# One set of PSUM banks, one order, one late pass for the low rows, and Strassen's products for batch 1 and the low rows

## The chip, the cores and the metric

The kernel runs on one core of a Trainium2 chip. The engines of that core are TensorE (PE in the profile, with its weight loads as PEld), VectorE (DVE), ScalarE (ACT), GpSimd (POOL) and SyncE (SP, which issues most DMAs). They run side by side and wait for each other by semaphores. The metric is the time of one execution on the device, in microseconds (us); lower is better.

## The reference

Two stages, for 8 batches. First an attention between 512 rows `x` and 32 rows `state` in 8 heads of width 64, in both directions; the results of both directions stand below each other, 544 rows of 512 values (the heads side by side) for each batch. Then a block of Fourier mixing with a two-layer network:

```python
scores  = scale * x @ state.T;  a  = softmax(scores);   xread = a @ state
scores2 = scale * state @ x.T;  a2 = softmax(scores2);  sread = a2 @ x
x = concat([xread, sread])                 # 544 rows of 512, per batch
u  = x + real(fft(fft(x, axis=rows), axis=columns))
un = (u - mean(u)) / sqrt(var(u) + 1e-6)   # per row
out = u + relu(un @ w_ch1) @ w_ch2         # 512 -> 2048 -> 512
```

All inputs and the output are float32.

## The kernel before

**Tiles and stages.** For each batch the 544 rows are 4 tiles of 128 rows and 32 rows more, the low rows (each batch has 32; the low rows of four batches make a tile of 128). A batch goes through: scores, transposed scores, reads of the state (`attend`, or `open_batch` for batch 0); the Fourier transform over the rows, made of products with cosine and sine tables (`over_s`, result tiles gp and G); the transform over the columns (`over_d`, `second_axis`, result yp); the sum U with the input; centring (ub) and transposing (unT); layer 1 (`layer1`: ph, then relu into hT); layer 2; and U plus the scaled result (ot), which is stored. Rows that have to be mirrored go by a buffer in DRAM (r_dram); low rows by l_dram.

**Layer 2** exists in two forms. `layer2` multiplies each 128-row tile of hT with w2: 16 matmuls of 512 columns into one bank po, then one step of VectorE. `layer2_fast` takes a pair of row tiles and treats hT (256 x 2048) and w2 (2048 x 512) as 2 x 2 blocks with Strassen's scheme in Winograd's form: seven products of 8 matmuls with 256 columns each instead of eight. For this it needs sums on both sides. The weight sums T1 to T4 are made once (`weight_sum`, VectorE). The sums of hT are made for each pair: S1 (tile SA), S2 (SB), and two that replace blocks of hT in place. The products gather in the banks poA and poB, and seven steps of VectorE (`put`) add them into ot. Before the change, batches 0 and 1 and the low rows use `layer2`, and batches 2 to 7 use `layer2_fast`.

**The low rows** are worked on twice: those of batches 0 to 3 in the step b = 3 of the main loop, those of batches 4 to 7 in b = 7 (`low_rows(g4)`), each with a pass of layer 1 (matmuls of 128 columns, tile unTL, result hTL) and of layer 2 of its own.

**Banks.** [...] The opening (batch 0's attention and its first transform) takes them from a pool ps0. After it the pool is closed, and psX (2 banks), psQ (3) and psF (3) are opened. At b = 3 these are closed again, and psX (2), psq (2) and psf (4) follow. BANKS says which bank each tile takes.

**Order.** The code doesn't issue instructions directly: a `Recorder` gathers them in groups, and `play` issues the groups in an order written out by hand or by a planner (ORDERS). `play` is called three times, so that there are three stretches: 0 (the opening, in the order of the code), 1 (up to b = 3) and 2 (the rest). No instruction moves across these borders. Groups of one key follow one another: the key of a TensorE instruction is the name of the tile that it writes.

**The opening**, ahead of which nothing runs: GpSimd makes index tables and clears buffers; VectorE and ScalarE turn them into the cosine and sine tables; SyncE and ScalarE load x of batch 0; TensorE fills its waits with small products that nobody reads (`warm`). Then come scores, exponentials (EE), reads, the fold of rows and columns (Sm, SS, XO0), the products gp, yp, U and ub. The first half of ub goes to ScalarE, the second to VectorE.

Every operation is issued by one helper, so the profile shows all at one line (L63); the tiles' names tell them apart.

Of the kernel before, what the change touches and what calls it, by code (L numbers as in the profile page):

```python
# [12 lines left out]
F32 = mybir.dt.float32  # L13
BF16 = mybir.dt.bfloat16
# [6 lines left out]
class Recorder:  # L21
# [4 lines left out]
    def __init__(self, nc):  # L26
        self.nc, self.groups, self.stretch = nc, [], 0
        for name in self.ENGINES:
            setattr(self, name, _Engine(self, name, getattr(nc, name)))
# [10 lines left out]
    def play(self):  # L40
        order = ORDERS.get(self.stretch) or range(len(self.groups))
        assert sorted(order) == list(range(len(self.groups)))
        for n in order:
            for call in self.groups[n][1]:
                made = call()
                if HOOK:
                    HOOK(self.stretch, n, made)
        self.groups, self.stretch = [], self.stretch + 1


class _Engine:
# [3 lines left out]
    def __getattr__(self, what):  # L55
        f = getattr(self._engine, what)
        if not callable(f):
            return f

        def call(*args, **kw):  # L60
            out = kw.get("out", args[0] if args else None)
            key = out.tensor.name if self._name == "tensor" else None
            self._rec.add(self._name, lambda: f(*args, **kw), key)  # L63

        return call


ORDERS = {n: [i for p in t.split() for i in range(int(p.split("-")[0]), int(p.split("-")[-1]) + 1)] for n, t in {
    1: """
        1-2 35 4 0 3 5-6 42 33 7 20 10 84 9 12-13 28 22 25 24 27 23 143 26 29 32 40 39 51 34 36 41 147 227 37 52-54 93 38 45 49  # L70
        57 50 58 43 61 87 63 55 46 62 64-65 47 70 105 48 71-72 88-89 148 18 73 123 76 80 21 82 11 15 209 74-75 19 78 16 210 77
        79 17 124-126 132 83 59 90 103 68 94 98 91-92 99 229 100 96 66 107 56 60 44 69 95 106 97 104 67 108-112 119-120 113 121
        118 114-116 152 117 145 157 165 159 161 101 85 175 182 167 173 169 158 146 166 160 162 102 176 168 174 170 86 171 180
        186 179 189 163 181 188 183-184 193 197 202 198 201 187 190 153 228 211 206 151 156 150 207 154 191 149 212 230 172 185
        164 199 195 200 224 222 235 194 203 215 218 223 295 196 208 192 81 283 14 122 281 130 279 128 231 213 232 129 233 214
        220 155 216 135 134 31 133 30 136 139-141 138 142 137 204 236 225 205 226 237 285 234 282 177 127 249 242 238 256 239
        245 296 243 287 240 246 244 251 250 221 144 262 252 261 260 253 259 265 450 255 254 263 451 266 302 270 288 267-269 286
        273 272 275 274 276 280 277-278 290 293 332 304 247 307 310 257 291-292 305-306 297 301 298 300 299 311-315 318-319 321
        320 323 327-328 324 330 309 374 326 334 339 337 316 335 322 329 341 343 346 241 303 271 178 333 294 248 308 325 375 331
        338 340 317 336 342 344 354 363 348 378 370 351 350 365 349 379 366 356-357 372-373 390-391 371 385 355 347 364 383 352  # L80
        361 381 384 353 386 369 382 360 394 389 397 362 217 258 264 455 377 376 396 395 449 454 431 402-403 411 404-405 419 430
        420 407 437 443 423 399 406 401 8 400 367 414 413 387 398 284 392 412 417-418 131 416 415 427 425 429 426 219 428 424
        289 446 478 456 421-422 409 444 432 436 445 435 439 457-458 434 433 459-461 472 474 469 464 468 465-466 473 467 537 481
        448 475 462 441 480 470 490 476 495 499 486 497 507 493 483 488 447 479 482 463 442 471 477 500 496 487 494 502 552 515
        550 510 527 549 511 557 542 485 509 491 503 518 504-506 517 519 516 558 556 498 484 508 489 553 524 532 551 539 531 523
        512-514 543 545 501 525 358-359 388 533 540 546-547 368 345 526 393 534 541 554 520 528 560 535 492 380 453 452 544 410
        522 530 538 559 438 440 408 529 521 561 536 555 548
    """,
    2: """
        38 2 13 0 12 4 1 36 8 97 22 32 5 61 9-10 37 39 14 23-24 98 62 46 11 15 17 16 19 18 21 20 44 63 131 65 56 53 33-34 42 7 6  # L90
        25 64 111 79 67 26 29 54-55 57 43 78 68 80 69 41 40 59 70 72 71 73-75 92 76 93 60 94 52 84 89 50 85 88 35 58 241 240 49
        47 82 48 83 51 86-87 30 104 113 99 175 95 90 123 106 115 102 119 117 125 45 183 132 112 31 77 96 103 120 110 108 121 188
        141 105 66 114 176 91 124 116 107 118 126 100 122 189 142 148 163 133 185 190 128 151 149-150 134 152 135-136 109 101
        225 177 138 145 143 161 200 144 129 137 164 154 191 186 140 178 139 146 155 147 201-202 158 208 162 166-167 221 217 174
        184 187 236 192 239 242 273 170 277 243 165 153 179 130 271 274-275 244-245 276 414 301 303 250 350 269 256 283 246 285
        223 203 159 204-205 212 210 27-28 211 213 168 215 214 156 216 226 218-219 209 222 230 206 227 237-238 194 229 263 228
        251 220 207 252-253 255 254 258-259 278 260 280 233 248 235 267-268 279 261-262 234 305 231 291 297 309 299 281 295 298
        249 282 304 171 351 270 257 284 361 286 224 180 247 306 232 292 300 302 296 264 311 287 320 342 265 313-314 366 362 330
        325 373 316 344 293 328 310 327 288 312 321-322 308 323-324 345 326 343 318 367 334 363 374 331 317 294 338 329 160 266
        272 332 195 356 399 364 358 368 169 413 157 379 315 380 394 359 357 319 369 333 197 416 290 352 337 360 346 193 415 417  # L100
        419 418 422 395 375 381 423 365 409 376-377 441 383 378 385 384 127 386 389 388 390 387 172 181 173 307 182 438 391 370
        407 392 371 393 396 408 439 443 410 397 509 448 468 424 450 470 528 444 398 510 339 347 451 469 471 411 400-401 412 403
        402 425-426 449 437 404 427-429 432 436 433 442 434 445 447 446 460 497 454 430 405 464 420 455 465 435 458 476 466 472
        492 462 461 431 406 498 459 353 467 473 421 463 523 452 487 540 478 529 535 533 511 477 475 489 488 490 480 479 491
        493-494 512 481-482 524 453 541 536 505 500 534 486 485 440 457 519 513 504 499 372 542 566 531 525 483 495 558 517 530
        484 496 518 501 543-544 532 526 567 348 354 335 545 551 336 502 474 340 553 355 557 552 554 349 556 341 503 555 537 577
        548 590 584 603 580 628 562 641 665 568 571 570 559 569 560 578 546 579 506 591 604 581 550 538 585-587 597 547 589 588
        593 605 574 610 572 564 582 592 561 563 607 575-576 594 596 583 595 606 618 673 624 622 598 630 626 608 625 601-602 599
        609 629 682 642 514 666 520 611 565 573 619 623 631 627 645 650 614 636 692 634 620 653 667 646-649 633 615 638 651 637
        635 639 652 640 668 656 674 661 693 643 621 644 654 657 662 515 521 632 516 699 685 679 683 686 701 700 689 612 687 456  # L110
        539 549 527 669 675 289 660 196 655 670 684 676 688 613 780 720 703 737 696 705 786 707 680 690 694-695 702 708 698 704
        711 507 677 671 658 678 663-664 659 522 508 709 672 710 718 712 748 713 719 725 714-715 729 722 730 723 81 681 617 691
        697 382 199 717 198 3 721 738 781 787 706 749 733 772 743 770 759 766 755 761 746 777 741 783 745 726 734 754 742 773
        744 716 771 767 762 756 760 778 784 739 731 750 727 752 757 747 753 758 768-769 732 740 751 728 801 774 779 782 798 785
        788 796 800 775 797 805 799 802 790 724 736 600 735 776 616 789 791 806 763 803 807 811 764 816 804 808 813 817 809 815
        812 821 810 814 822 819 823 818 820 824-826 833 827 831 834 828 836-837 765 794 793 792 835 795 829 839 830 840 838 832
        841
    """,
}.items()}
BANKS = {  # L120
    "psQ":
        "210002012201120210210201120120221012000022121021",
    "psF":
        "1220102100210012220120212011120210020012002110100101102212",
# [8 lines left out]
HOOK = None  # L133
# [1419 lines left out]
```

## Time and profile before

| | us |
|---|---|
| median of three runs | 294.81 |
| lowest and highest | 293.24, 295.10 |
| the profiled execution | 294.75 |
| its span, from the first to the last instruction | 293.0 |

| engine | busy us | share of the span | instructions |
|---|---|---|---|
| TensorE | 280.3 | 96% | 2599 |
| TensorE weight loads | 193.1 | 66% | 2599 |
| VectorE | 207.0 | 71% | 530 |
| ScalarE | 164.7 | 56% | 323 |
| GpSimd | 98.1 | 33% | 227 |

The span is the part of the time that the trace covers; 1.75 us lie around it. A share of busy time is a mean over stages, so it is read together with the row that cuts the span into 40 slices and with the chain of waits, which follows the work that ended last back to the start. A row of a group of instructions gives its busy time, the mean duration of one in ns, and the idle time of the engine ahead of them with what ended it. Matmuls overlap, so their mean duration is longer than their spacing; the spacing is read from the chain.

### The profile page before, as it was taken

What the parts mean: (1) busy time and instruction counts of PE and PEld (TensorE: products, weight loads), DVE (VectorE), ACT (ScalarE), POOL (GpSimd) and SP (SyncE); (2) the same over time, 40 slices, a digit from 0 to 9 for tenths busy, and PEclk for the clock granted to TensorE, in tenths of its full rate; (3) what the DMA queues carried; (4) which work ended last, traced back from release to release, by engine and by line L of the source; (5) the groups of instructions that cost most, each with busy time, mean ns of one, the idle gap of its engine ahead of it and who ended that gap; (6) DMA issues with size and microseconds to landing.
All of it is one profiled execution on the core that took longest, in us unless ns stands there. A gap on an engine that the chain in (4) does not pass through costs nothing.

```text
span 293.0 us, 6742 instructions
## 1 busy us (share of the span) xinstructions
PE 280.3 (96%) x2599; PEld 193.1 (66%) x2599; DVE 207.0 (71%) x530; ACT 164.7 (56%) x323; POOL 98.1 (33%) x227
## 2 busy tenths in 40 slices
PE   5997999999999999999999999999999999999993
PEld 4677987554654546677764867767666866768682
DVE  8878696449579955895569795986787964613772
ACT  6984755764763696346845647276766584253000
POOL 6762683628057127600243011611273106000000
PEclk9997999999999999999999999999999999999998
DMA  9999499599934547855356034721352058640655
GB/s 159 190 203 212 77 154 110 115 172 163 196 80 103 101 121 140 180 121 140 66 118 127 25 94 123 120 72 39 70 122 61 22 107 187 136 110 0 130 160 143
DMA packets 110972, 34.91 MB, mean 119 GB/s; under 512 B 101996, under 2 KB 106476, under 8 KB 110940
## 3 DMA queue, kind: packets, MB, share of 16 engines
q1 hardware_dynamic: 100220, 28.72, 47.0%
q0 software_dynamic: 4224, 4.19, 9.2%
q10 hardware_dynamic: 6496, 1.57, 2.6%
q8 instruction: 20, 0.33, 0.5%
q14 instruction: 12, 0.10, 0.1%
HBM read 22.41 MB, written 14.02 MB: 124 GB/s over the span
## 4 chain that ended last, share of the span: by engine, by line
PE 72%; DVE 10%; SPq 6%; DMA 4%; POOL 3%; ACT 1%; issue 1%; DVEq 0%; POOLq 0%
PE ph L63 31%; PE poA L63 14%; PE poB L63 10%; PE po L63 7%; SPq L63 6%; PE gp L63 3%; PE yp L63 2%; DMA xT<-xin 2%; DMA xs<-in_x_dram 2%; DVE U L63 1%; DVE XR L63 1%; PE eTp L63 1%; DVE SS L63 1%; PE esp L63 1%; DVE XQ L63 1%
## 5 line engine op out<-in xcount | busy, mean ns | idle before, releaser
L63 PE MATMUL ph<-unT,w 128*128 128x512 bf16 (+1 forms) x704 | 124.9, 324 | 1.0 <-DVE unT L63 0.4
L63 ACT ACTIVATE hT<-ph 128x512 bf16<-128x512 f32 x128 | 74.4, 596 | 63.1 <-PE ph L63 62.9
L63 PEld LDWEIGHTS <-w 128*128 128x128 bf16 x832 | 66.2, 99 | 42.3 <-issue 1.1
L63 PEld LDWEIGHTS <-hT 128*128 128x128 bf16 x616 | 58.7, 98 | 22.1 <-issue 0.2
L63 POOL CAST xin<-xs 128x2048 bf16<-128x2048 f32 (+3 forms) x14 | 14.3, 1044 | 53.7 <-DMA xs<-in_x_dram 36.3
L63 PE MATMUL po<-w,hT 128*128 128x512 bf16 x128 | 30.4, 379 | 0.0
L63 DVE SCALAR_TENSOR_TENSOR ot<-poA,rstd,U 128x256 f32<-128x256 f32 (+1 forms) x37 | 17.1, 471 | 13.2 <-PE poA L63 11.4
L63 PE MATMUL poB<-w,hT 128*128 128x256 bf16 x192 | 24.9, 273 | 0.0
L63 POOL TENSOR_TENSOR rstd<-rstd,mhalf 128x1 f32<-128x1 f32 x34 | 21.8, 650 | 0.5
L63 ACT CAST G<-gp 128x288 bf16<-128x288 f32 (+2 forms) x31 | 13.5, 480 | 9.1 <-PE gp L63 8.7
L63 ACT ACTIVATE ub<-U,S 128x512 bf16<-128x512 f32 (+1 forms) x22 | 15.1, 705 | 4.1 <-DVE U L63 3.1
L63 POOL COPY XT<-XR 32x514 bf16<-32x514 bf16 x7 | 4.6, 661 | 32.7 <-DVE rcs L63 16.6
L63 POOL TENSOR_SCALAR rstd<-ssq 128x1 f32<-128x1 f32 x20 | 5.2, 258 | 30.7 <-ACT junk L63 29.8
L63 ACT ACTIVATE junk<-U,S 128x512 bf16<-128x512 f32 x20 | 14.3, 715 | 0.6 <-DVE S L63 0.4
L63 DVE SCALAR_TENSOR_TENSOR U<-yp,XF 128x510 f32<-128x510 f32 (+1 forms) x24 | 10.0, 421 | 5.6 <-PE yp L63 5.3
L63 DVE TENSOR_TENSOR SA<-hT 128x1024 bf16<-128x1024 bf16 x12 | 8.2, 681 | 7.1 <-ACT hT L63 6.6
L63 DVE SCALAR_TENSOR_TENSOR ot<-poB,rstd,ot 128x256 f32<-128x256 f32 x24 | 11.5, 480 | 2.2 <-PE poB L63 1.7
L63 DVE TENSOR_TENSOR hT<-hT,SB 128x1024 bf16<-128x1024 bf16 x12 | 8.7, 726 | 5.9 <-PE poB L63 5.8
L63 PE MATMUL poA<-TB,hT 128*128 128x256 bf16 (+1 forms) x104 | 12.5, 264 | 0.1
L63 PE MATMUL poA<-w,hT 128*128 128x256 bf16 x96 | 12.4, 273 | 0.0
L63 PE MATMUL poA<-TA,SB 128*128 128x256 bf16 x96 | 12.4, 273 | 0.0
L63 PE MATMUL poB<-TA,SA 128*128 128x256 bf16 x96 | 12.4, 273 | 0.0
(188 smaller groups left out, 483.5 us busy)
## 6 DMA issues: line engine op xcount, KB each, us to landing
xs<-in_x_dram SPq DMA_DIRECT2D x22, 256.0 KB, 4.0
w<-in_moe_w_ch_dram POOLq DMA_DIRECT2D x8, 512.0 KB, 9.4
out_dram<-ot SPq DMA_DIRECT2D x15, 256.0 KB, 3.4
r_dram<-ot SPq DMA_DIRECT2D x14, 256.0 KB, 2.9
out_dram<-r_dram SPq DMA_DIRECT2D x14, 256.0 KB, 3.8
xs<-in_x_dram SPq DMA_DIRECT2D x8, 192.0 KB, 2.8
xs<-in_x_dram ACTq DMA_DIRECT2D x2, 256.0 KB
l_dram<-ot SPq DMA_DIRECT2D x2, 256.0 KB, 2.2
```

Of the source, the lines that this page charges most:

```text
L63: self._rec.add(self._name, lambda: f(*args, **kw), key)
```

## The change

1. **One set of banks.** psX (2 banks) and psB (6 banks) are opened at the start and stay. Every tile that came from ps0, psQ or psF now comes from psB with a new list of banks; a few tiles of the opening (the warm products, sTp, srp, hdp) use the two banks of psX.
2. **One order.** `play` is called once at the end, with one list ORDER for all 1,678 groups, the opening included. The key of a TensorE group now also holds which bank of a two-bank tile is written.
3. **Low rows in one late pass.** `low_rows()` runs once, at b = 7, on both tiles of 128; layer 1 takes 256 columns at once, and hT of the low rows (hTL) lies in a buffer of the x loads.
4. **Strassen's products for batch 1 and the low rows.** `layer2` is left to batch 0. The weight sums are made earlier: T1 and T2 at the end of b = 1, T3 and T4 at the start of b = 2 (before: all in the second half of b = 2). T3 moves out of the buffer stb into TB, T4 into a buffer that held the states (TC), and SA gets a buffer of its own.

The lists of the order and of the banks are left out below, as are the lines that only rename a pool.

```diff
     def play(self):
-        order = ORDERS.get(self.stretch) or range(len(self.groups))
+        order = ORDER or range(len(self.groups))
...
-            key = out.tensor.name if self._name == "tensor" else None
+            key = (out.tensor.name, out.offset // 512 % 2) if self._name == "tensor" else None
...
-    opening = ExitStack()
-    ps0 = opening.enter_context(tc.tile_pool(name="ps0", bufs=1, space=bass.MemoryType.PSUM))
+    psX = ctx.enter_context(tc.tile_pool(name="psX", bufs=1, space=bass.MemoryType.PSUM))
+    psB = Banks(tc, ctx, "psB", 6)
...
-    def low_rows(g4):
-        key = ("L", g4)
-        unT = wk.tile([128, DC, 128], BF16, name="unTL", tag="unTL", bufs=1)
...
+    def low_rows():
+        key = "L"
+        unT = un_of[key] = wk.tile([128, DC, 512], BF16, name="unT", tag="unT", bufs=2)[:, :, 0:256]
+        U = wk.tile([128, 2, 514], F32, name="U", tag="U", bufs=5)
+        tiles = tiles_of[key] = []
+        rstds, ubs = [], []
+
+        def over_d(g):
+            yp = second_axis([GLs[g][:, c, :] for c in range(4)])
+            add_forward(U[:, g, 0:512], yp, XLs[g][:, 0:512])
+
+        def centre(g):
+            mv, rstd = stats_of(U[:, g, 0:512], "rstd")
+            rstds.append(rstd)
+            ubs.append(wk.tile([128, 512], BF16, name="ub", tag="ub", bufs=5))
+            nc.vector.tensor_scalar(ubs[g], in0=U[:, g, 0:512], scalar1=mv[:, 0:1], scalar2=None, op0=ALU.subtract)
+
+        def turn_u(g):
+            nc.sync.dma_start_transpose(out=unT[:, :, 128 * g:128 * g + 128], in_=ubs[g])
+            tiles.append((U[:, g, 0:512], lambda: rstds[g], g))
+
+        return [lambda g=g, f=f: f(g) for g in range(2) for f in (over_d, centre, turn_u)]
...
     def layer1(key):
-        low = isinstance(key, tuple)
-        n = 128 if low else 512
-        hT = wk.tile([128, FC, n], BF16, name="hTL" if low else "hT", tag="hTL" if low else "hT", bufs=1 if low else 2)
+        n = 256 if key == "L" else 512
+        if key == "L":
+            hT = wk.tile([128, 4 * dm], F32, name="hTL", tag="xs").bitcast(BF16).rearrange("p (f n) -> p f n", n=n)
+        else:
+            hT = wk.tile([128, FC, n], BF16, name="hT", tag="hT", bufs=2)
...
     def prepare_sums():
         strassen["T"].append(wk.tile([128, 4, S], BF16, name="TB", tag="xT").rearrange("p a s -> p (a s)").rearrange("p (f n) -> p f n", n=256))
-        strassen["S"] = [wk.tile([128, 4, 2, 128], BF16, name="SA", tag="E").rearrange("p a b c -> p (a b) c"),
+        strassen["T"].append(wk.tile([128, 1024], F32, name="TC4", tag="gen3", bufs=1).bitcast(BF16).rearrange("p (f n) -> p f n", n=256))
+        strassen["S"] = [wk.tile([128, 8, 128], BF16, name="SA", tag="SA", bufs=1),
...
+        if key == "L":
+            return pair(0)[1]
         (s0, p0), (s1, p1) = pair(0), pair(1)
...
     for b in range(1, B + 1):
-        if b == 3:
-            nc.play()
-            middle.close()
-            psX = ctx.enter_context(tc.tile_pool(name="psX", bufs=1, space=bass.MemoryType.PSUM))
-            psQ, psF = Banks(tc, ctx, "psq", 2), Banks(tc, ctx, "psf", 4)
         reads_next = reads_after
-        l2, l2_now = (layer2(b), [l2[7]] + l2[8:]) if b == 1 else (None, l2 if b == 2 else layer2_fast(b - 1))
+        l2, l2_now = (None, [l2[7]] + l2[8:] if b == 1 else layer2_fast(b - 1))
         early, until, start = {2: (8, 0.28, 0.25), 3: (3, 0.13, 0.1)}.get(b, (0, 0, 0.08))
-        l2_now = l2_now + (layer2(("L", b // 4)) if b in (3, 7) else [])
+        if b == B - 1:
+            low, low1 = low_rows(), layer1("L")
+            l2_now = l2_now + layer2_fast("L")
...
         if b == 2:
-            prepare_sums()
-            streams.append(([lambda i=i: weight_sum(i) for i in range(4)], 0.5, 1))
+            streams.append(([lambda i=i: weight_sum(i) for i in (2, 3)], 0.02, 0.2))
...
-        if b in (3, 7):
-            streams.append((low_rows(b // 4), 0.02, 0.2))
-            streams.append((layer1(("L", b // 4)), 0.36, 0.8))
+        if b == B - 1:
+            streams.append((low, 0.02, 0.3))
+            streams.append((low1, 0.36, 0.7))
         weave(*streams)
     nc.play()
```

With all groups counted, the change leaves 2,607 matmuls where there were 2,599, and 64 of the 160 po matmuls. In the opening's new order the clears of stb, XN, XF and XR come early on GpSimd, ahead of or between the index tables; SyncE's first loads are a 15-row piece of x(0), the state, three more pieces of x(0), a piece of x(1), and then the 96-row piece of x(0); on VectorE the casts of x(0) come ahead of the copy of sT, and the second index table (second_table) comes after the first reads.

## The prediction

> **What bounds the kernel now.** I read the page first: busy shares and slices, then the chain.
>
> ```profile
> PE 280.3 (96%) x2599; PEld 193.1 (66%) x2599; DVE 207.0 (71%) x530; ACT 164.7 (56%) x323; POOL 98.1 (33%) x227
> ...
> PE   5997999999999999999999999999999999999993
> ...
> PEclk9997999999999999999999999999999999999998
> ...
> PE 72%; DVE 10%; SPq 6%; DMA 4%; POOL 3%; ACT 1%; issue 1%; DVEq 0%; POOLq 0%
> ```
>
> TensorE (PE) is full in all slices (7.3 us each) but three: 0, 3 and 39. A busy PE is not yet PE at its peak, so I took the true spacing of matmuls from the chain of waits (start, us, what):
>
> ```profile
> 14.84 3.82 PE gp L63 x39
> 20.06 1.31 DVE U L63 x4
> 21.37 1.79 DVE ub L63
> 24.15 1.86 PE ph L63 x16
> 26.87 1.27 PE ph L63 x16
> 29.07 0.89 PE ph L63 x16
> ...
> 84.25 2.59 PE po L63 x12
> ...
> 268.39 0.87 PE poB L63 x8
> ```
>
> 2.59/12 is 0.216 us for a 512-column matmul, 0.87/8 is 0.109 for 256 columns, 0.89/16 is 0.056 for 128. With these, all matmuls from the first layer-1 product of batch 0 (24.15) on sum to 262.0 us, and PE's last one ends at 288.0: 263.8 us for 262.0 of work. From 24 us on nothing but matmul columns counts. Ahead of it lie 24.2 us of opening, behind it 5.0 us in which only the last rows are stored. The chain's first lines show the opening: gp products, U, ub, then a first ph at half speed (1.86 for 16).
>
> The opening's worst wait, in the order of time of VectorE (DVE):
>
> ```profile
> 20.68 0.68 DVE L63 SCALAR_TENSOR_TENSOR U<-yp,XF 128x510 f32<-128x510 f32 x1
> 21.29 0.08 DVE L63 DVE_READ_ACCUMULATOR U<-yp,XF 128x1 f32 x1
> 21.29 1.88 DVE L63 TENSOR_SCALAR ub<-U,S 128x256 bf16<-128x256 f32 x1
> ```
>
> 1.88 us for 256 columns, where the 512-column form of the same row takes 0.48 (group by shape), while GpSimd (POOL) clears buffers from 21.39 to 22.87.
>
> [...] granted clock 0.91 over 20 to 25 us and 0.75 over 25 to 30, which is 3.4 us at half speed, some 1.7 us of work lost. [...]
>
> **The change part by part.** The sum is made against the profiled execution: 294.75 us, span 293.0 and 1.75 around it (the median of three runs is 294.81).
>
> 1. Layer 2 of batch 1. Removed 64 matmuls of 512 columns (half of the po row below), 64 × 0.216 = 13.8 us; added 2 pairs × 7 products × 8 of 256 columns, 112 × 0.109 = 12.2. **−1.6** on the bound engine.
> 2. Low rows. Layer 2: 32 × 0.216 = 6.9 becomes 56 × 0.109 = 6.1, −0.8. Layer 1: 128 × 0.056 = 7.2 becomes 64 of 256 columns, 7.0, −0.2. **−1.0.** The four stores to the l_dram buffer and their readers are as many as before (2 and 8 transfers), only the first half moves to the end. ScalarE (ACT) still does 8 evictions.
>
> ```profile
> L63 PE MATMUL po<-w,hT 128*128 128x512 bf16 x128 | 30.4, 379 | 0.0
> ...
> L63 DVE SCALAR_TENSOR_TENSOR ot<-poA,rstd,U 128x256 f32<-128x256 f32 x35 | 16.5, 478 | 13.2 <-PE poA L63 11.4 <-POOL rstd L63 1.2 <-DMA l_dram<-ot 0.6
> ...
> L63 PE MATMUL ph<-unTL,w 128*128 128x128 bf16 x128 | 8.3, 219 | 0.0
> ...
> L63 PE MATMUL po<-w,hTL 128*128 128x512 bf16 x32 | 7.6, 379 | 0.0
> ...
> L63 DVE TENSOR_TENSOR SA<-hT 128x1024 bf16<-128x1024 bf16 x12 | 8.2, 681 | 7.1 <-ACT hT L63 6.6
> ```
>
> 3. VectorE pays for it: each new pair has 4 sums of 0.70 and 7 combining steps of 0.48, 6.2 us; three pairs 18.5, less 6 steps of 0.75 that go: **+14.0 of VectorE work**. Two thirds (12.3 less 4 × 0.75, so +9.3) fall on batches 1 and 2, and the four weight sums (1.22 each, 98.7 to 110.9 now) come earlier there too. By windows (PE, PEld, DVE, ACT, POOL busy):
>
> ```profile
> 80.00:85.00 5.00, 5.00 (x60) 2.62 (x59) 4.76 (x13) 3.53 (x7) 1.19 (x1) 1.00 0.44 87
> ...
> 90.00:95.00 5.00, 5.00 (x26) 2.37 (x25) 4.81 (x10) 2.25 (x4) 3.44 (x9) 1.00 0.34 69
> 95.00:100.00 5.00, 5.00 (x35) 2.70 (x33) 4.83 (x12) 2.39 (x6) 0.00 (x0) 1.00 0.74 98
> ```
>
> Over 60 to 120 us VectorE is busy 44.5 of 60 us; it becomes about 54. PE hides that only if each sum precedes its product. Where it is tightest, after batch 3's last read of its state, the new order puts 10.6 us of PE work ahead of the first product that needs T1 and S1, and 10.5 us of VectorE work ahead of those. There the cover is nearly gone; late next would be the second S2, then T4. I take **+0.5** of PE waits, 0 to 3 as bounds.
>
> 4. Banks and one order. The pools no longer close twice, so no new bank waits for an old pool; six banks serve all. PE's idle time between 40 and 140 us is 1.4 us in five pieces (0.19, 0.29, 0.16, 0.25, 0.54); two of them are transposed loads that come late and may stay. I take **−0.2**; bounds −1.0 and +1.5, since the order of every queue changes, SP's loads included.
>
> 5. The opening, now reordered as well. The clears of stb, XN and the like move to POOL's start; just before ub POOL has only casts and short clears, started by the same fold as now, some 2.7 us of work; the fold ends more than 3 us ahead of ub, so POOL should be through. So ub's half should fall from 1.88 to about 0.3: −1.6. The 510-column U step moves behind ub: −0.6. Against it: the first scores now come after three casts and the copy of sT, not after the first one. VectorE from 6.85 (7.25 less the 0.4 table step, moved) + 3 × 0.42 + 2 × 0.41 + scores 0.4 gives the first exp at about 9.6 instead of 8.64; VectorE's chain to the fold (7.2 us now) follows at that lag: +1.0. Also a 1.0 us clear goes ahead of the identity on POOL, so the PE warm-up starts some 1.4 us later, covered by the wait for x; and the 96-row piece of x(0), second on SP now, is seventh[...], and behind it queue batch 1's rows: 0 to +0.7. The state load is second on SP, +0.5, covered by the same wait. First weights: POOL issues two of them about as early, the third and fourth 2 us later, at 14 and 15 us; with the median 9.4 us from issue to landing they are there by 25, and needed from 26 on. Net **−1.2**; bounds −2.6 (no lag) and +1.5 (lag twice as large, block stays). The half-clock window is kept; if it goes, −1.4 more.
>
> 6. The end. After the last layer-1 product there are 22 products of 0.87, 19.2 us, against 19 and two of 1.73, 20.0, now (part of 1 and 2). VectorE has some 16.7 us there, so it keeps up. SP issues eight low-row transfers there, not four; the last two stores wait 2.2 us for landing, then four issues of 0.8: free some 3 us before PE's end. 0, at most +0.5.
>
> Sum: −2.6 + 0.5 − 0.2 − 1.2 = −3.5: **291.2 us**.
>
> **The rivals.**
> *Only the columns go.* The late scores eat what ub gains, and stalls of 0.3 remain: 294.75 − 2.6 + 0.3 = 292.4. For it: the chain of the opening is VectorE's without a gap from 9.7 to 16.9. Against it: PE worked off gp products until 18.7, and these now start earlier (XB is folded first), so part of the lag is hidden.
> *Everything falls into place*: no half-speed window, half of the middle's 1.4 us of gaps gone (0.7, of which 0.2 is counted already): 291.2 − 1.4 − 0.5 − 0.5 (no waits for sums) = 288.8. For it: PE's gap of 1.6 us before 23.2 is what likely sets the window off.
> *VectorE becomes the bound* in batch 1's pairs, **slower than before**. [...] It decides once PE's waits for sums exceed the 3.8 us of parts 1, 2 and 5. At four such places (two pairs of batch 1, batch 2's first pair, the low pair) 1.7 us each gives 6.8 less 3.8: 297.8. For it: slices of 4.8 in 5. Against it: before 60 us and after 105 VectorE has room (2.4 in 5 over 105 to 115).
> *The change doesn't do what it says*: the program holds the 112 and 56 products, so this is out; only the clock could hide them.
>
> **How the numbers follow.** A measurement here can tell about 1% (2.95 us) from no change, as the three runs span 0.6%. Forecast case 0.48 (289.6 to 292.8; four fifths faster by over 1%), only the columns 0.31 (291.5 to 294; mostly within), all in place 0.12 (faster), VectorE-bound 0.09 (294.5 to 299; mostly slower). That gives faster 0.55, within 0.37, slower 0.08. The range 288.5 to 294.3 leaves out some 0.06 below (the best of all in place) and 0.1 above.
>
> **What would show it.** The po row at 64, no unTL row, 168 more poA and poB matmuls; PE busy some 3 us shorter. ub's 256-column step near 0.3 us; first ph near 23.0. VectorE near 219 us. PE idle between 25 and 287 below 2 us, with waits for SA, SB, TA or hT short. If idle PE time for those exceeds 3 us, part 3 was wrong; if the first ph comes after 24.2, part 5.

## The result and the profile after

| | us |
|---|---|
| kernel before, median of 20 runs beside the changed one | 293.49 |
| changed kernel, median of 20 runs (294.56 to 296.13) | 295.19 |
| ratio, with its 95% interval | 1.0048 (1.0033 to 1.0064) |
| predicted | 291.2 (288.5 to 294.3) |

The changed kernel takes 0.5% longer. Its profiled execution took 295.05 us, its span 293.3. The page (busy times; the span in 40 slices, each 7.3 us) says that the saving is there, and where it was lost:

```profile
PE 276.9 (94%) x2607; PEld 197.9 (67%) x2607; DVE 214.1 (73%) x557; ACT 161.7 (55%) x323; POOL 98.2 (33%) x227
...
PE   3499999999999999999999999999999999999992
...
PEclk9999999999999999999999999999999999999999
```

TensorE is busy 3.4 us less than before (280.3). That isn't the columns alone: the half-clock window, which made TensorE busy some 1.7 us longer in the execution before (granted clock 0.50 from 24.12 to 27.53 us), is gone too, and ahead of the first layer-1 product it is busy about 1 us longer than before. From slice 2 to the last but one it is full, and the mean granted clock of the execution is 1.00. But its first two slices fell from 5 and 9 tenths to 3 and 4. The opening got longer. The changed kernel's order of time (start, duration, engine, what; in brackets the idle time before it and what ended it) shows where:

```profile
1.98 0.06 DVE L62 MEMSET stb<- 32x4 bf16 x1
...
6.34 0.17 DVE L62 CAST pf<-pi__89 128x7 f32<-128x7 int32 x1 [4.30 <-PE xTp L62]
6.36 0.07 DVE L62 MEMSET xin<- 128x8 bf16 x1
...
10.21 0.68 ACT L62 ACTIVATE TS<-gen 128x576 bf16<-128x576 f32 x1 [4.05 <-DVE gen L62]
...
27.80 0.35 DVE L62 TENSOR_SCALAR ub<-U,S 128x256 bf16<-128x256 f32 x1
...
29.14 1.05 PE L62 MATMUL ph<-unT,w 128*128 128x128 bf16 x16 [0.39 <-DVE unT L62]
```

VectorE does nothing from 2.04 to 6.34 us, and what ends its wait is a product of TensorE, the transposes of x (xTp). The instruction that waits is the small memset in the second row (the rows overlap by a few hundredths): it writes the ones columns of x's first bf16 buffer. The casts of x fill columns 1 to 512 of that buffer and the memset only columns 0 and 513, but in the program it waits for the cast and the transposes issued ahead of it. In the kernel before it was VectorE's first instruction, and VectorE came to the tables without a wait:

```profile
0.81 0.10 DVE L63 MEMSET xin<- 128x8 bf16 x2 [0.81 <-PEq L1537]
...
5.74 0.68 ACT L63 ACTIVATE TS<-gen 128x576 bf16<-128x576 f32 x1 [0.57 <-DVE gen L63]
```

In the new order (where it is group 25) it stands behind ScalarE's cast of x's third tile and TensorE's transposes of it. All of VectorE's table work queues behind it, ScalarE waits 4.05 us for the tables, and so on down the opening.

The stations of the opening and the rest of the span, from the order of time, with one experiment beside them (below):

| us | before | changed | changed, memset first |
|---|---|---|---|
| sine table begins (ScalarE) | 5.74 | 10.21 | 6.37 |
| first cast of x on VectorE | 7.25 | 10.83 | 7.03 |
| first exponential | 8.64 | 14.59 | 10.00 |
| yp | 19.36 | 25.90 | 20.60 |
| first layer-1 product (ph) | 24.15 | 29.14 | 23.85 |
| from there to the start of the last rows' products | 261.62 | 256.50 | 256.46 |
| from there to the end of the span | 7.23 | 7.66 | 7.69 |
| span | 293.0 | 293.3 | 288.0 |

So the change gained 5.1 us between the first layer-1 product and the last rows, lost 5.0 ahead of them and 0.4 behind them.

### The profile page after: what moved, and what is told of

Read it like the earlier page. It is cut to its first block, busy times and chain, and to the rows that moved or that the text cites. A ratio compares the mean times of both kernels' runs of the same rounds, so it can differ in the third digit from the quotient of the medians.

```text
span 293.3 us, 6792 instructions
## 1 busy us (share of the span) xinstructions
PE 276.9 (94%) x2607; PEld 197.9 (67%) x2607; DVE 214.1 (73%) x557; ACT 161.7 (55%) x323; POOL 98.2 (33%) x227
## 4 chain that ended last, share of the span: by engine, by line
PE 89%; DVE 6%; DMA 1%; POOL 1%; issue 1%; ACT 0%; SPq 0%; DVEq 0%
PE ph L62 39%; PE poA L62 17%; PE poB L62 13%; PE po L62 5%; PE gp L62 4%; PE yp L62 2%; PE esp L62 2%; PE xrp L62 1%; PE eTp L62 1%; DVE XR L62 1%; DVE gen L62 1%; PE xfp L62 1%; DMA gen<-in_state_dram 1%; DVE ot L62 1%; PE srp L62 1%
## 5 line engine op out<-in xcount | busy, mean ns | idle before, releaser
L62 PE MATMUL ph<-unT,w 128*128 128x512 bf16 (+2 forms) x768 | 129.8, 317 | 0.5 <-DVE unT L62 0.4
L62 ACT ACTIVATE hT<-ph 128x512 bf16<-128x512 f32 x128 | 70.9, 597 | 69.7 <-PE ph L62 69.4
L62 DVE SCALAR_TENSOR_TENSOR ot<-poA,rstd,U 128x256 f32<-128x256 f32 (+1 forms) x46 | 21.4, 472 | 17.1 <-PE poA L62 16.9
L62 PE MATMUL poB<-w,hT 128*128 128x256 bf16 x224 | 28.5, 273 | 0.0
L62 POOL TENSOR_TENSOR rstd<-mv,epst 128x1 f32<-128x1 f32 x14 | 3.7, 272 | 40.9 <-DVE mv L62 37.9
L62 PE MATMUL po<-w,hT 128*128 128x512 bf16 x64 | 15.1, 379 | 0.0
L62 PE MATMUL poA<-TC,hT 128*128 128x256 bf16 (+1 forms) x120 | 14.5, 265 | 0.1
L62 PE MATMUL poA<-TB,hT 128*128 128x256 bf16 x112 | 14.3, 273 | 0.0
L62 PEld LDWEIGHTS <-SB 128*128 128x128 bf16 x120 | 11.6, 98 | 2.4
L62 DVE SCALAR_TENSOR_TENSOR U<-yp,XF 128x2 f32<-128x2 f32 (+1 forms) x24 | 10.0, 421 | 4.2 <-PE yp L62 3.5
```

## The experiments

Times of runs are compared with the kernel before on the same chip: 293.75, 293.99, 293.49 and 294.1 us in the four sets, so runs of different sets can differ by some tenths for that reason alone. `move(groups, ahead_of)` takes groups (numbers in ORDER) out of the order and puts them ahead of another one.

### One memset, both ways

```diff
+move([25], 27)        # changed kernel: the memset stands first on VectorE
```

> The changed kernel with one memset moved in VectorE's order: the one that writes the ones columns of x's first bf16 buffer (group 25) stands first on VectorE again, ahead of the table work, and no longer behind the cast and the transposes of x's third tile. Theory (that memset waits 4.3 us, and the tables, casts and scores queue behind it): VectorE's 4.3 us wait is gone, the cosine and sine tables start near 6 us, not 10.2, the first layer-1 product comes near 25 instead of 29.1, and the time falls by about 4, to 291. Second theory (the wait is only half of it, because the 96-row piece of x is issued seventh on SyncE and lands near 8.5): the casts of x start near 8.5 instead of 10.8, first layer-1 product near 26.8, time near 293. Rival (the opening is bound by the order of the casts or by clears on GpSimd, and the wait is covered): first layer-1 product later than 28.5, time 295.

Measured: 289.79 us, ratio to before 0.987 (0.9843 to 0.9896), 5.4 less than the changed kernel. The first of the three expectations held, and by more than it said. The wait is gone, and with it the delay behind it:

```profile
0.81 0.07 DVE L62 MEMSET xin<- 128x8 bf16 x1 [0.81 <-PEq L1535]
...
6.37 0.68 ACT L62 ACTIVATE TS<-gen 128x576 bf16<-128x576 f32 x1
...
10.00 1.57 ACT L62 ACTIVATE EE<-esp 128x512 bf16<-128x512 f32 x3 [0.27 <-PE esp L62]
...
23.85 1.05 PE L62 MATMUL ph<-unT,w 128*128 128x128 bf16 x16 [0.39 <-DVE unT L62]
```

The piece of x issued seventh didn't hold the casts (the first begins at 7.03). More came back than the wait of 4.30: the sine table is 3.84 earlier, two casts of x on VectorE take 0.43 each instead of 0.86 and 0.70, and the first layer-1 product is 5.29 earlier; the rest isn't accounted for. One instruction of 0.07 us, moved, turns a loss of 0.5% into a gain of 1.3%. The reverse, in the kernel before (the list also moves groups of other engines, but in the queues only this memset changes its place):

```diff
+ORDERS[0] = [*range(25), *range(26, 43), 86, 87, 89, 90, 25, *range(43, 86), 88, *range(91, 218)]
```

> The kernel before the change, with only the same memset put late on VectorE: behind the cast and the transposes of x's third tile and ahead of the table work. Theory: VectorE waits some 3.5 us there, the first layer-1 product moves from 24.2 to about 27.5, and the time rises by 3 to 3.5, to about 297. Rival (the opening of the kernel before has other bounds, such as the loads of x and the state, which hide it): first layer-1 product within 1 us of 24.2, time within 1 of the kernel before.

Measured: 298.75 us, ratio 1.0175 (1.0141 to 1.0209), 5.0 more. Its order of time has the same picture:

```profile
6.17 0.17 DVE L63 CAST pf<-pi__71 128x7 f32<-128x7 int32 x1 [4.20 <-PE xTp L63]
...
28.60 1.05 PE L63 MATMUL ph<-unT,w 128*128 128x128 bf16 x16 [0.42 <-DVE unT L63]
```

The first layer-1 product comes 4.45 later for a wait of 4.20. The expected 3 to 3.5 was too little: nothing in that opening takes up any of the delay. The time rose by 5.0, and what it has above 4.45 may be something else: five of these six executions show a mean granted clock of 0.994 or less, against 7 of 31 of the kernel before, and in the profiled one the clock is 0.66 from 10 to 15 us. In both directions the memset's place is worth 4.5 to 5.4 us.

### The other changes in the opening

```diff
+move([25], 27)
+move([19], 23)         # 96-row piece of x: third on SyncE
+move([13, 14], 12)     # identity ahead on GpSimd
+move([87, 90], 96)     # copies of sT and xT ahead of VectorE's casts
```

> As the run with the memset first, and three more parts of the opening put as they were before the change: the 96-row piece of x goes third on SyncE instead of seventh, the identity is made ahead of GpSimd's other tables and clears, and the copies of the transposed state and of x's first transposed tile stand ahead of VectorE's three casts of x. If the rest of the change is worth what the trace says (some 5 us after the first layer-1 product), first layer-1 product near 24, time near 290. If these three parts cost nothing in the changed kernel, the same as the run with the memset first, within 0.5. Rival (the gain after the opening came only from a start that was later, with loads and clears long done): first layer-1 product at 24 to 25, but the time stays at 293 or above, because waits appear behind it.

Measured: 292.14 us, first layer-1 product at 26.66. Putting three more parts back cost 2.35 against the run with the memset first, where about the same time was expected. The rival that looked for waits behind the opening fell too: from the first layer-1 product to the last rows it took 256.46 us, as in the run with the memset first. The parts one by one:

> The changed kernel with the memset first, and of the three parts put back in the run with the opening as before only one: the copies of the transposed state and of x's first transposed tile stand ahead of VectorE's three casts of x. Theory (the copy waits for TensorE's transposes of the state, the casts queue behind it, and in the pause TensorE falls back to half its rate, so that 13 idle products take 1.4 us instead of 0.9): the casts start near 8.4 instead of 7.0, the first layer-1 product near 26, time 291.5 to 292.2, nearly all of the 2.35 us by which that run was longer. Prediction's own view (late casts and scores cost 1.0, so this order is the better one): time 289 or less. Rival (the identity or the piece of x was the cause): 289.8 within 0.3.

(Edit: groups 25 and 87, 90 only.) Measured: 292.26 us, first layer-1 product at 26.48: all of it. The order of time of that run, and below it its chain of waits (start, us, what):

```profile
8.05 0.42 DVE L62 COPY sT<-warm 128x512 bf16<-128x512 bf16 x1 [1.06 <-PE warm L62]
8.40 0.42 DVE L62 COPY xT<-xTp 128x512 bf16<-128x512 bf16 x1
8.73 0.42 DVE L62 CAST xin<-xs 128x512 bf16<-128x512 f32 x1
```

```profile
12.86 1.39 PE warm L62 x13
```

A copy at the head of VectorE's queue waits 1.06 us for TensorE, and the cast behind it, which could have run, starts at 8.73 instead of 7.03. TensorE in turn lacks transposes, and is idle for 1.19 us ahead of 9.21. After that pause its 13 idle products take 0.107 us each (1.39/13), against 0.056 in the run with the memset first (0.73/13, from 10.52 to 11.25).

> The changed kernel with the memset first, and the other two parts: the 96-row piece of x third on SyncE instead of seventh, and the identity ahead of GpSimd's other tables and clears. The prediction held the late identity for covered by the wait for x, and the late piece of x for 0 to +0.7. If so: time 289.0 to 289.8. Rival (the identity ahead makes VectorE's tables late by 0.5, and four idle products at 2.2 are wasted because TensorE has paused again by the time x is there): first layer-1 product 24.4 to 26.7, time 290.3 to 292.

(Edit: groups 25, 19 and 13, 14 only.) Measured: 290.25 us, first layer-1 product at 24.35, between the two expectations and nearer to the rival: an early identity and an early piece of x bring nothing, and the tables come 0.2 later (sine table at 6.57). That they stand late in the new order costs nothing, as the prediction had it for the identity.

### The kernel before: TensorE's pause, and the blocked step

```diff
     copies1[2]()
-    warm(4)
+    warm(30)
```

> The kernel before the change, with 30 instead of 4 idle products of TensorE ahead of the transposes of ub, so that 1.4 of the 1.6 us in which TensorE waits for ub's second half are filled. Theory (the half-clock window behind it is set off by that gap): granted clock 1.00 over 24 to 28 us, time lower by 1.4 to 1.7, near 292. Rival (the window has another cause, or comes and goes from run to run): the window is still there, or the time stays within 0.5 of the kernel before.

Measured: 292.92 us, ratio 0.9973 (0.996 to 0.9986). By windows (busy PE, PEld, DVE, ACT, POOL; then the granted clock), first the kernel before, then this one:

```profile
20.00:25.00 5.00, 3.00 (x41) 2.65 (x40) 4.94 (x12) 2.55 (x5) 3.45 (x9) 0.91 1.23 204
25.00:30.00 5.00, 5.00 (x104) 4.88 (x103) 2.85 (x10) 3.15 (x8) 0.00 (x0) 0.75 1.11 209
```

```profile
20.00:25.00 5.00, 4.58 (x79) 4.27 (x77) 4.95 (x12) 2.55 (x5) 3.59 (x9) 1.00 1.24 209
25.00:30.00 5.00, 4.98 (x118) 4.55 (x116) 4.01 (x15) 4.01 (x10) 0.07 (x1) 1.00 1.17 211
```

The half-clock window is gone with the pause. But the gain is 0.8, not 1.4, and the list of runs says why: of 31 runs of the kernel before in this set, 7 show a mean granted clock of 0.994 or less (median 294.9 us), 24 a higher one (median 293.4); of the 22 runs of this kernel none is below 0.995. (By an estimate from the span of 293 us, 3.4 us at half clock lower the mean to 0.994; where in the span they lie, the mean doesn't tell.) In the other three sets it is 14 of 28, 6 of 27 and 4 of 11 runs. So a mean that fits the window comes in about one execution in three, and the profiled one of before, on which the prediction's sum stood, was one of them (0.990; besides the window it has a clock of 0.68 from 290 to 291 us and of 0.50 in the last 2 us, where TensorE is idle). Even against the 24 runs with a higher mean this kernel is 0.5 us shorter; the cause of that isn't shown.

```diff
+ORDERS[1].remove(4)                              # ub's half on VectorE ...
+ORDERS[1].insert(ORDERS[1].index(35), 4)         # ... ahead of the 510-column step of U
```

> The kernel before the change with one swap on VectorE: ub's half stands ahead of the 510-column step of U, as in the changed kernel, so that it runs before GpSimd's clears begin at 21.4. Theory (the 1.88 us of that step are its block by the clears): the step falls to 0.3, the first layer-1 product comes 1.2 to 1.5 earlier, near 22.8, the time falls by 1.2 to 1.5, to 292.2; TensorE's wait for ub shrinks too, so the half-clock window behind it should no longer show. Rival (the block moves to the U steps that now run beside the clears, and the copies behind them): the first layer-1 product within 0.3 of 24.15, the same time.

Measured: 292.68 us, ratio 0.9942 (0.9923 to 0.996), a little short of what the theory said. The step of ub, now just ahead of the first clear, took 0.63 us instead of 1.88, the first layer-1 product came at 23.08 instead of 24.15, and the mean granted clock of that execution was 0.997 instead of 0.990:

```profile
20.85 0.63 DVE L63 TENSOR_SCALAR ub<-U,S 128x256 bf16<-128x256 f32 x1
...
21.43 0.32 POOL L63 MEMSET XQl<- 128x256 f32 x1
```

The U steps, now beside the clears, took 0.67 and 0.68 as before, so the block didn't move to them. Part of the 1.3 us in time goes with the half-clock window; none of the 15 runs has a mean granted clock below 0.995, and against the 14 of 28 runs of the kernel before with a mean above 0.994 (median 293.4) the swap gains 0.8.

### Is VectorE a bound?

```diff
+move([25], 27)
+TWICE = {606, 627, 640, 651}          # the groups of T1 to T4; the second run adds 632, 633, 655, 656, 812, 813, 867, 868
...
-            for call in self.groups[n][1]:
+            for call in self.groups[n][1] * (2 if n in TWICE else 1):
```

> The changed kernel with the memset first, and with each of the four weight sums T1 to T4 made twice in a row, 4 x 1.22 = 4.9 us of VectorE work more between 80 and 110 us, where VectorE is busiest (19.45 of 20 us over 80 to 100). Rival of the prediction (VectorE is the bound there, or at its edge): the time rises by most of it, 3 to 5 us, to 293 to 295, and TensorE shows waits for sums (SA, SB, T) or for banks. Theory (TensorE still has cover ahead of each sum): at most 1 us, 290 to 290.8.

> As the run with the weight sums twice, and the first two sums S1 and S2 of the four pairs of batches 1 and 2 made twice too: 8 x 0.68 = 5.4 us more, 10.3 in all, over some 60 us, in which VectorE has some 11 us idle. Theory: part of it can't be hidden, since VectorE's idle time lies at other places than the sums: 1 to 4 us, 291 to 294. Rival (VectorE is the bound there): 8 to 10 us, 298 to 300. If even this costs under 1 us, VectorE was far from being the bound.

Measured: 294.28 us, ratio 1.0015 (0.9992 to 1.0037), and 299.61 us, ratio 1.0192 (1.0148 to 1.0235). From the first layer-1 product to the last rows that is 261.29 and 265.95 us against 256.46: 4.8 us for 4.9 us of added sums (4 × 1.22), 9.5 for 10.4. The rival's numbers came, not the theory's. With the weight sums twice, TensorE's list of waits (us in total, times, the longest) now names sums (TB, TA) and combining steps (ot):

```profile
PE poA L62 <- DVE TB L62: 1.0, 1, 1.0
PE yp L62 <- DVE ot L62: 1.0, 1, 1.0
PE poB L62 <- DVE ot L62: 0.7, 2, 0.6
...
PE poB L62 <- DVE TA L62: 0.3, 1, 0.3
...
PE poA L62 <- DVE TA L62: 0.2, 1, 0.2
```

By windows, the run with the memset first, then the one with the weight sums twice:

```profile
95.00:100.00 5.00, 5.00 (x46) 3.75 (x45) 4.96 (x14) 1.91 (x5) 0.00 (x0) 1.00 0.74 146
100.00:105.00 5.00, 5.00 (x51) 4.28 (x50) 4.25 (x12) 2.73 (x6) 0.00 (x0) 1.00 0.39 99
```

```profile
95.00:100.00 5.00, 4.10 (x31) 3.00 (x32) 4.93 (x11) 0.36 (x1) 0.00 (x0) 1.00 0.64 131
100.00:105.00 5.00, 3.73 (x41) 2.69 (x40) 4.97 (x8) 3.92 (x8) 0.00 (x0) 1.00 0.21 32
```

In the first run both engines are full in the earlier window (VectorE has 0.04 us left) and TensorE doesn't wait; in the later one VectorE has 0.75 left. In the second run VectorE is full in both, and TensorE loses 0.9 and 1.3 us. So VectorE is at its edge there without costing anything yet: in this order a sum that comes later is paid for nearly in full. What another order could make of the same work, the runs don't show.

### Small moves that brought nothing

> The changed kernel with the memset first, and three small moves in the opening that bring the first scores forward: the index tables that VectorE waits for go ahead of the other iota on GpSimd, the copy of x's first transposed tile goes ahead of the third cast on VectorE, and the first scores go ahead of the third tile's transposes on TensorE. Theory (the prediction's term of +1.0 for late scores is real, and the chain from the first exponential to the fold follows it): first exponential near 9.3 instead of 10.0, first layer-1 product 0.4 to 0.7 earlier, near 23.3, time near 289.3. Rival (the chain goes by the last exponential, or by the tables): first exponential earlier, first layer-1 product and time the same within 0.2.

(`move([25], 27)`, `move([43], 47)`, `move([1, 8, 5, 7], 12)`, `move([90], 97)`, `move([93], 111)`.) Measured: 289.89 us. The first exponential came at 9.62 instead of 10.00, yp at 20.62 as before that: the rival held.

> The run with the first scores sooner, and in addition the 13 idle products of TensorE that stand ahead of the first sums of the exponentials and of the fourth scores go behind them. That run moved the first exponential by 0.4 and nothing behind it, which speaks for the later exponentials as the chain's link. Theory (the chain goes by the third exponential's sums and the fourth scores, which wait behind the idle products): first reciprocal near 10.9 instead of 11.4, fourth exponential near 11.2 instead of 11.7, first layer-1 product near 23.4 instead of 23.9, time near 289.4. Rival (the chain goes by VectorE's and GpSimd's own work from the first reads on): first layer-1 product within 0.2 of 23.9, time within 0.3 of 289.8.

(In addition `move([88, 92], 126)`.) Measured: 290.06 us, first layer-1 product at 24.23. The theory fell: the first reciprocal moved by -0.09 against the run with the memset first, and yp came 0.4 later. The rival's time held, but not its first layer-1 product.

> The changed kernel with the memset first, and ub's half put right behind the first step of U on VectorE, ahead of two short clears of the state buffer and of a 2-column step of U that the new order has put in between. In the run with the memset first these three took 0.3 to 0.4 us between yp and the first layer-1 product, which were not in the prediction's sum (it counted -1.6 for ub's half and -0.6 for the 510-column step). Theory (VectorE's short steps stand on the path here): first layer-1 product 0.3 to 0.4 earlier, near 23.5, time near 289.5. Rival (GpSimd's clears, which run until 22.8, then block ub's half at its new, earlier place, as before the change): ub's half takes 0.6 us or more instead of 0.35, first layer-1 product within 0.15 of 23.85 or later.

(`move([25], 27)`, `move([375], 379)`, `move([221], 375)`.) Measured: 290.25 us. The theory fell, and the rival's reason with it: ub's half took 0.37 us and wasn't blocked. Its order of time:

```profile
22.22 0.51 ACT L62 ACTIVATE ub<-U,S 128x256 bf16<-128x256 f32 x1 [1.15 <-DVE U L62]
22.22 0.37 DVE L62 TENSOR_SCALAR ub<-U,S 128x256 bf16<-128x256 f32 x1
...
24.10 1.05 PE L62 MATMUL ph<-unT,w 128*128 128x128 bf16 x16 [0.67 <-DVE unT L62]
```

The transposes need ScalarE's half of ub as well, and that takes 0.51 and ends at 22.73. With the memset first, ScalarE's half ended at 22.78 and VectorE's at 22.86, so VectorE lost almost nothing by its short steps ahead of ub. Moved behind it, they push the copy of unT, and the first layer-1 product comes 0.25 later.

None of these moves beats the changed kernel with the memset first, which stays 1.3% below the kernel before and 1.8% below the changed one (289.79 against 295.19).

## Why the prediction was wrong

**The step that failed is part 5, the opening:** "Net −1.2; bounds −2.6 (no lag) and +1.5". It was +5.0, from 24.15 to 29.14. By the prediction's own test ("if the first ph comes after 24.2, part 5") it failed. Its working took VectorE's time of 6.85 for the first cast from the trace of before and put the new order of casts and copies behind it. It didn't walk VectorE's new queue from its first instruction, with the waits of each, and so put the memset's wait at nothing. There the memset stands behind the transposes of x, at the price of 4.3 us of wait, and with no work on VectorE that could hide it; the first cast came at 10.83. Both single moves of that memset show this: 5.4 us back in the changed kernel, 5.0 lost in the kernel before. No rival had it: the one that ended slower put the loss in VectorE's work of batch 1.

Without the memset the rest of part 5 is 23.85 against 24.15, -0.3 instead of -1.2:
- *Late scores, +1.0:* yp came 1.24 late, near the forecast, but as a sum of other terms, so that is luck. VectorE's first reciprocal behind the exponentials is 1.85 late (11.55 against 9.70). From there to the last step of the fold VectorE takes 8.40 us, without a wait of 0.2 us, where it took 7.22. And less is left of the products gp behind the fold: from its end to yp it is 0.65 instead of 2.44. Together that is 1.85 + 1.18 - 1.79 = 1.24. The prediction had the chain at its old length, and the part that is hidden only in a rival. Its reason isn't borne out either: a first exponential 0.38 earlier doesn't move yp, and the old order of casts and copies costs 2.5 in this opening, so the casts first are a gain. The tables start 0.63 later; what else holds up the first reciprocal stays open.
- *ub's half and the U step, -1.6 and -0.6:* yp to the first layer-1 product fell from 4.79 to 3.25 us, -1.54. That is the step of ub alone, which went from 1.88 to 0.35 as forecast. That its length goes with GpSimd's clears is shown by the swap in the kernel before: 1.88 us beside them, 0.63 just ahead of them, and the first layer-1 product 1.07 earlier. What in the clears lengthens it isn't shown. The -0.6 didn't come: with short steps in the place of the 510-column one, the way from the start of U to ub is only 0.26 shorter (0.97 against 1.23), and U starts 0.24 later after yp.
- *Identity and piece of x:* the identity was covered, as said; the piece of x cost nothing, the low end of 0 to +0.7.

**Parts 1, 2 and 4 were right.** The four weight sums and the pairs are there, and po stands at 64 products. From the first layer-1 product to the last rows the change saves 5.1 us. The half-clock window of the profiled execution before is 1.9 of it (261.62 against 259.68 with the pause filled). The other 3.2 are 2.7 of TensorE's busy time (258.42 with the pause filled, 255.72 after) and 0.5 of its idle time (1.26 and 0.78); the prediction had 2.6 and 0.2. Its sum of 262.0 us for all columns is some 1.4 too high, since with the pause filled TensorE needs 261.9 us for them, idle time included; the difference of the two kernels doesn't suffer from that.

**Part 3** (+0.5, 0 to 3) came out at the low end: the list of TensorE's waits in the changed kernel (all of 0.2 us and more) names no sum, neither SA, SB nor a T. The added steps of VectorE come to 14.1 us, as forecast (8.9 of sums, 9.8 of combining steps less 4.6 that went), but its busy time rose only to 214.1 and not to the 219 of the signs: other steps got shorter, ub's by 1.5, and the page counts time in which two steps overlap only once. It was also right about the place ("there the cover is nearly gone"): the runs with doubled sums pay for nearly every added microsecond.

**Part 6** (0, at most +0.5) measured 0.43.

**The half-clock window** was to stay. It is in none of the changed kernel's slices, and of its 20 executions none has a mean granted clock below 0.995. In the kernel before, too, it differs from run to run: a mean that fits it is in 31 of the 97 runs of the four sets. So a sum made against one execution that holds the window starts 1.3 us above the median of before (294.75 against 293.49).

With the memset in its old place, the forecast of 291.2 would have stood against a measured 289.8. That it comes so near is in part luck: of the 5.0 us between the two spans (293.0 and 288.0) 1.9 are the window, which the sum had kept, and the opening gave 0.3 instead of 1.2.

## What to carry to other kernels

When an order is replaced, walk each engine's queue anew from its first instruction and write beside each one the last thing that it waits for; times taken over from the old trace hold only up to the first new wait. Here an instruction of 0.07 us handed its wait of 4.30 us on to all that stood behind it in the queue, and the wait came from a tile that it shares with others rather than from data that it needs. The chain of tables and casts at the start had no cover in this kernel, so look there first.

## What the runs showed of the hardware

- TensorE's slow phase in the opening doesn't show in the granted clock: in the run with the casts behind, the window from 12 to 14 us has a granted clock of 1.00 while idle products of 128 columns follow one another at 0.107 us. TensorE takes up work again at 9.21, after 1.19 us without any, and the idle products are slow until 14.25, some 5 us later. With the memset first TensorE is idle for 0.11 us in all from 6 to 11 us, and the same products come at 0.056 us.
- Pauses of 1.58 and 0.43 us, close together, stand ahead of a stretch of 3.4 us at a granted clock of 0.50 in the profiled execution of the kernel before. A mean granted clock that fits such a window is in 31 of 97 executions of that kernel, in none of 22 with 1.4 us of the pause filled with idle products, and in none of 15 where the swap of ub leaves one pause of 1.03 us.
- A cast of x on VectorE took 0.86 us beside two clears of GpSimd in the changed kernel, 0.70 beside GpSimd's issuing of a weight load and a cast, and 0.43 with the memset first, where GpSimd did next to nothing meanwhile. ub's half, 0.35 where GpSimd did little beside it, took 0.63 beside the issuing of a weight load. None of these was tested by itself.
